# Attention and expert layer on one core: idle products and another split of work at the hand-over to the first expert

## The chip, the cores and the metric

The kernel runs on one core of a Trainium2 chip. The core has a matrix engine (TensorE, PE in the profile; its weight loads are PEld), three engines for elementwise work (VectorE or DVE, ScalarE or ACT, GpSimd or POOL), an engine that mostly issues transfers (SyncE, SP), and sixteen DMA engines that move data between device memory (DRAM) and on-chip memory (SBUF). Matrix products land in PSUM, which has eight banks. Each engine works through its own list of instructions in the order in which the program issued them; it waits at an instruction until the semaphores that the instruction names have been reached, and everything behind it waits too.

The metric is the device time of one execution in microseconds (us), lower is better.

## The reference

The reference has two parts. The first is an attention with a threshold for 8 batches, 8 heads, 576 tokens and head size 64; the second sends each of the 8 x 576 = 4608 tokens to one of 8 experts, with room for exactly 576 tokens each:

```python
scores = scale * np.matmul(q, k.transpose(0, 1, 3, 2))
thresh = np.max(scores, axis=-1, keepdims=True) - tau
scores = np.where(scores >= thresh, scores, -1000000000.0)
attn = softmax(scores)                       # exp, divided by its sum + 1e-9
x = (attn @ v) laid out as 4608 rows of 512

logits = x @ w_gate                          # 4608 x 8
# all 36864 logits in falling order: a token goes to the expert of its first
# logit whose expert still has room (576 tokens each)
for e in range(8):
    h = np.maximum(x[assigned == e] @ w1[e], 0.0)     # 512 -> 1024
    out[assigned == e] = h @ w2[e]                    # 1024 -> 512
```

## The kernel before, in words

**Attention** (lines 23 to 386) fills the first 483 us. It ends with thirty transposes of attention's result into rows of 512 values and 8 factors (`xt_unit`, lines 241 to 251; 520 values in all). PE transposes into a bank `xo`, ScalarE copies to `pp`, and SP's queue stores the rows into the DRAM tensor `xrows`. The factors are the reciprocals of the softmax sums: the rows are stored unscaled.

**The router** (class `Router`, from line 429) finds which expert fills up first and its 576 tokens, then the next, eight times. One such phase searches for a threshold in seven rounds. In each round DVE compares (`step_cmp`, tile `cmp`), PE counts (`step_cnt`, line 493), DVE copies the counts (`cn`), PE adds them (`step_flag`, line 499), DVE makes flags (`jka`), and PE turns them into the next threshold (`step_n`, lines 515 to 529). Then the expert is picked, its tokens are ranked (`rank1`, `rank2`, lines 561 to 577) and the list of the 576 rows is packed (`pack`, lines 662 to 677; tile `idx`). For the first expert nothing else is left to do beside it, which the flag `alone` marks. PE products that nobody reads are issued there by `warm` (lines 624 to 627): 20, 4 and 50 by `WARM`, all into columns 256 to 383 of the bank `rps`, which also receives the search's results. A second bank, `cps`, receives the compaction.

**The experts** (`moe`, from line 683) run one after another. Expert number r has these parts:

- `w1_load` (lines 705 to 735) loads the first weight matrix (four transfers of 128 rows of 1024 into `w1s`), on ScalarE's queue for r = 0, otherwise on SP's. The products need single passes of a rounded type, so each value is held as a high part and a low part: ScalarE makes the high part `w1h`, DVE subtracts it from the original and so makes the low part `w1l`. For r = 0 DVE makes the low parts in four groups of 128-column blocks: block 0, block 1, blocks 2 and 3, blocks 4 to 7.
- `w2_load` (lines 736 to 751) does the same for the second matrix on SP's queue (`w2s`, `w2h`, `w2l`), with the low parts put on a list of spare work for DVE (`later`, line 695).
- `rows` (lines 753 to 812) gathers the 576 rows in five blocks (four of 128, one of 64) by indirect transfers that GpSimd issues (line 759, tile `xg`), scales them by their factors (`scale`, line 762, on DVE; for r = 0 block 2 by eight ScalarE instructions, `scale_act`, line 767), transposes them on PE (`turn`, line 785), and splits the result into high and low parts (`xh` by ScalarE in line 786, `xl` by DVE in `low`, line 787).
- `ffn` (lines 814 to 884) multiplies. Layer 1 has eight blocks f of 128 hidden columns. Each needs 12 pairs of products: 4 row groups k, times high by high, low rows by high weights, high rows by low weights (line 840); a pair covers the two column halves of the 576 tokens. For r = 0 the halves are 256 and 320 tokens wide, the three kinds follow one another, and blocks 0 and 1 do their first half before either does its second, so that they can start with the first two row blocks alone. ScalarE then applies the Relu (`hf`, `H`), and DVE makes the low part of H. Layer 2 (line 872) follows, then the results are stored by indirect transfers of GpSimd (line 879), with one addition on GpSimd per expert (line 882).

**What sets the order.** A planner written in Python runs when the program is built. Each part is a generator that yields an estimated time; `run` (line 920) keeps a clock and issues, in order of the estimated times, what is due, between the products of the current expert. So the search for expert 1 is woven into the products of expert 0. Each `yield` number is such a time. The order of each engine's list is fixed by this; the waits come from the data. The tuple ("w1", 0) in `done` marks that the high parts of expert 0 are issued, ("half", 0) that two row blocks are, ("x", 0) that all are.

DVE's instructions all carry line 425, since they pass through a helper; they are told apart by their tiles.

Of the kernel before, what the change touches and what calls it, by code (L numbers as in the profile page):

```python
# [9 lines left out]
F32 = mybir.dt.float32  # L10
# [3 lines left out]
AF = mybir.ActivationFunctionType  # L14
ALU = mybir.AluOpType
# [413 lines left out]
class Router:  # L429
# [191 lines left out]
        u2=wk.tile([128,NC_],F32,name="u2"); V.scalar_tensor_tensor(u2,s.sc,BIGS+CAP,u,op0=ALU.is_lt,op1=ALU.mult)  # L621
        V.tensor_tensor(L,L,u2.unsqueeze(2).to_broadcast([128,NC_,8]),op=ALU.add)
    def close(s): s.close1(); s.close2()
    def warm(s,n):

        ps=s.ps()
        for i in range(n): s.T.matmul(ps[:,256:384],s.ones,s.tri,start=True,stop=True)
    def phase(s,last=False):

        s.stage="search"; V=s.V  # L630
        def held(t): s.pe=t; V.after(V.now+t+0.2)
        if s.first: s.prep(33)
        else:
            yield V.ease()
            s.prep()
            yield V.ease()
        s.alone=s.first; s.first=False
        if last:

            lo=s.wk.tile([128,1],F32,name="lo"); V.memset(lo,-FMAX/4); E={"lo":lo}  # L640
        else:
            E={"E":s.k("E1"),"lv":-1}
            def gap():

                w=V.wait(); s.fill()
                return w
            s.on=True
            for i in range(7):
                s.step_cmp(E); yield gap()
                held(0.34); s.step_cnt(); yield gap()  # L650
                held(0.16); s.step_flag(E["lv"]); yield gap()
                held(0.1); E=s.step_n(E)
                if not s.alone: yield V.ease()
            s.on=False
        s.pick(E)
        if last:
            yield V.wait()
            held(0.13); s.pick2()
        s.stage="pick"; s.rank1(E)
        yield V.wait()  # L660
        held(0.2); s.rank2()
# [16 lines left out]

LATS=[0.15,0.35,0.7]+[0.8]*5; FIX=(0.125,0.15)
GA=[5.0,6.5,8.0,8.0]; AGE=7.0; HALF=1; WARM=[20,4,50]  # L680
W1Y=5.0; L2O=(0,4,1,2,3); L2Z=1; HFB=3; RW=[0.2,0.4,0.4,0.4]; LOWP=(); LPF=7; LOWT=1.4; PREPW=1; WLY=(1.0,1.0)

def moe(ctx,tc,R,start,xrows,w1,w2,out,ident):
    nc=tc.nc
    V=R.V; A=nc.scalar; G=nc.gpsimd; T=nc.tensor
    E,D,F=w1.shape
# [8 lines left out]
    def later(k,g): fills.append((clk[0],k,g))  # L695
# [9 lines left out]
    def w1_load(r,s):  # L705
        while r>0 and ("w1a",r-1) not in done: yield 0.5
        q=nc.scalar if r==0 else nc.sync
        s["e"]=q.value_load(s["ei"][0:1,0:1],min_val=0,max_val=E-1)
        for k in range(4):
            t=w1p.tile([128,F],F32,name="w1s",bufs=4); s["w1s",k]=t  # L710
            q.dma_start(t,w1[ds(s["e"],1),k*128:(k+1)*128,:].rearrange("o p f -> p (o f)"))
        yield W1Y if r==0 else 5.0
        while r>0 and ("l1",r-1) not in done: yield 0.5
        s["w1h"]=w1p.tile([128,4,F],F32R,name="w1h"); s["w1l"]=w1p.tile([128,4,F],F32R,name="w1l")
        if r==0:
            for k in range(4):
                A.activation(s["w1h"][:,k],s["w1s",k],AF.Copy); yield 1.1
            done.add(("w1",0))
            for a,b in ((0,1),(1,2),(2,4),(4,8)):
                while (("row",0,1),"scaled",("row",0,4))[min(a,2)] not in done: yield 0.1  # L720
                o=slice(128*a,128*b)
                for k in range(4):
                    V.tensor_tensor(s["w1l"][:,k,o],s["w1s",k][:,o],s["w1h"][:,k,o].bitcast(F32),op=ALU.subtract)
                    if a>1: yield 0.9 if a<4 else 2.0
                for f in range(a,b): done.add(("w1l",f))
            done.add(("w1a",0))
            return
        def lowpart(k,o): V.tensor_tensor(s["w1l"][:,k,o],s["w1s",k][:,o],s["w1h"][:,k,o].bitcast(F32),op=ALU.subtract)
        for c in range(2):
            for k in range(4):  # L730
                o=slice(c*F//2,(c+1)*F//2)
                A.activation(s["w1h"][:,k,o],s["w1s",k][:,o],AF.Copy)
                yield WLY[0]
                later(("w1" if c==0 else "w1a",r) if k==3 else ("w1p",r,c,k),lambda k=k,o=o: lowpart(k,o))
                yield WLY[1]
    def w2_load(r,s):
        while ("g",r) not in done or (r>0 and ("w2",r-1) not in done): yield 0.5
        e=nc.sync.value_load(s["ei2"][0:1,0:1],min_val=0,max_val=E-1)
        for k in range(4):
            t=wk.tile([128,2,D],F32,name="w2s",bufs=4); s["w2s",k]=t  # L740
            nc.sync.dma_start(t,w2[ds(e,1),k*256:(k+1)*256,:].rearrange("o (k p) d -> p (o k) d",p=128))
        yield 5.0
        while ("w1a",r) not in done or (r==0 and ("x",0) not in done) or (r>0 and ("l2",r-1) not in done): yield 0.5
        s["w2h"]=wk.tile([128,8,D],F32R,name="w2h"); s["w2l"]=wk.tile([128,8,D],F32R,name="w2l")
        def lowpart(k,c): V.tensor_tensor(s["w2l"][:,2*k+c],s["w2s",k][:,c],s["w2h"][:,2*k+c].bitcast(F32),op=ALU.subtract)
        for k in range(4):
            for c in range(2):
                A.activation(s["w2h"][:,2*k+c],s["w2s",k][:,c],AF.Copy)
                yield WLY[0]
                later(("w2l",r,2*k+c) if 2*k+c<7 else ("w2",r),lambda k=k,c=c: lowpart(k,c))  # L750
                yield WLY[1]

    def rows(r,s):
        while r>0 and ("x",r-1) not in done: yield 0.5
        order=(4,0,1,2,3) if 0<r<=HALF else range(5)
        for t in order:
            n=128 if t<4 else 64
            x=wk.tile([128,XW],F32,name="xg",bufs=5); s["xg",t]=x
            G.indirect_dma_start(out=x[:n],out_offset=None,in_=xrows,in_offset=IOA(ap=s["idx"][:n,t:t+1],axis=0))
        s["ei2"]=wk.tile([128,1],I32,name="ei2",bufs=2); G.tensor_copy(s["ei2"],s["ei"])  # L760
        done.add(("g",r))
        def scale(t):

            n=128 if t<4 else 64
            v=s["xg",t][:n,:D].rearrange("p (h d) -> p h d",h=8)
            V.tensor_tensor(v,v,s["xg",t][:n,D:XW].unsqueeze(2).to_broadcast([n,8,64]),op=ALU.mult)
        def scale_act(t):
            x=s["xg",t]
            for h in range(8): A.activation(x[:,64*h:64*h+64],x[:,64*h:64*h+64],AF.Copy,scale=x[:,D+h:D+h+1])
        if r==0:  # L770
            step0=R.phase(); R.ahead=step0
            for _ in range(3): next(step0)
        yield GA[min(r,3)]
        while r>0 and ("l1",r-1) not in done: yield 0.5
        s["xh"]=wk.tile([128,4,576],F32R,name="xh"); s["xl"]=wk.tile([128,4,576],F32R,name="xl")
        def parts(t):
            ps=s["xps",t]
            if r==0: return (lambda n: s[n][:,:,128*t:128*t+128] if t<4 else s[n][:,:,512:576]),ps if t<4 else ps[:,:,:64]
            if t<4: return (lambda n: s[n][:,:,128*t+32*(t//2):128*t+32*(t//2)+128]),ps
            return (lambda n: s[n].rearrange("p k (a b) -> p k a b",a=2)[:,:,:,256:288]),ps[:,:,:64].rearrange("p k (a b) -> p k a b",a=2)  # L780
        def turn(t):
            n=128 if t<4 else 64
            ps=pt.tile([128,4,128],F32,name="pt"); s["xps",t]=ps
            held[0]+=0.5
            for d in range(4): T.transpose(ps[:,d,:n],s["xg",t][:n,d*128:(d+1)*128],ident[:n,:n])  # L785
            xv,pv=parts(t); A.activation(xv("xh"),pv,AF.Copy)  # L786
        def low(t):
            xv,pv=parts(t)
            V.tensor_tensor(xv("xl"),pv,xv("xh").bitcast(F32),op=ALU.subtract)
            done.add(("row",r,t))  # L790
            if t==1: done.add(("half",r))
        if r==0:


            def step(n=1):
                for _ in range(n): next(R.ahead)
            step(); scale(0); step(); turn(0); scale(1); low(0); turn(1); scale_act(2); yield V.ease()
            low(1); yield 0.25
            scale(3); scale(4); done.add("scaled"); yield 1.8
            turn(2); yield 0.6  # L800
            turn(3); low(2); yield 0.6
            turn(4); low(3); yield 0.6
            low(4); done.add("ahead")
            done.add(("x",0)); return
        scale(order[0]); yield V.wait()
        for i,t in enumerate(order):
            turn(t)
            if i<4: scale(order[i+1])
            yield max(0.8,V.wait())
            low(t)  # L810
            yield RW[min(r,3)]
        done.add(("x",r))
# [197 lines left out]
```

## Time and profile before

| | |
|---|---|
| median of 3 runs | 992.01 us (991.7 to 992.86) |
| profiled execution | 990.17 us |
| its span, first to last instruction | 988.4 us |
| PE busy | 949.5 us, 96% |
| DVE, ACT, POOL busy | 765.2, 636.3, 275.9 us |
| mean granted clock of PE | 0.990 |
| data moved | 117.01 MB, mean 118 GB/s |

A row of a timeline gives start and duration in us, the engine, the line of the kernel, the operation, output and inputs by the program's names, the shape (partitions x elements) and the number of instructions merged into the row; brackets give the idle time of the engine just before and what ended it. "SPq" and "ACTq" are transfers being issued on these queues. A row of busy time by slice gives the stretch and its length, then the busy time of each engine with its number of instructions, the granted clock of PE as a share of full speed, the busy share of the DMA engines, and GB/s. In a row of grouped instructions the columns after the bar are the total busy time and the mean duration in ns.

### The profile page before, as it was taken

To read this page: it belongs to the slowest core of one execution; us is meant where nothing else is said; L and a number is where in the kernel's file an instruction comes from. 1 tells how busy PE (TensorE), PEld (TensorE's weight loads), DVE (VectorE), ACT (ScalarE), POOL (GpSimd) and SP (SyncE) were. 2 spreads that over 40 slices of the span, in tenths; PEclk is the share of its full clock that TensorE was granted. 3 is DMA by queue.
4 is the path that set the end of the run, shared out by engine and by line. 5 is a ranking of instruction groups with operands and counts; after the bars stand their busy time and mean duration, and the time that the engine had idled before them with its cause. 6 is when DMAs were issued, how large, how long until landed. Compare 5 with 4: busy or idle time off the path is not lost.

```text
span 988.4 us, 24280 instructions
## 1 busy us (share of the span) xinstructions
PE 949.5 (96%) x9235; PEld 706.1 (71%) x9235; DVE 765.2 (77%) x2100; ACT 636.3 (64%) x1287; POOL 275.9 (28%) x460
## 2 busy tenths in 40 slices
PE   6999999999999999998889999999999999999996
PEld 4566656665666665665688797887978879898995
DVE  7999999999999999995678887686886786535220
ACT  6899899999999999996554354342543434545340
POOL 2334444443434343340110302222204023210202
PEclk9999999999999999999889999999999999999998
DMA  6231532642533333206732524151514335341101
GB/s 253 97 107 40 181 110 95 218 149 75 189 97 113 122 103 117 85 3 228 256 125 97 166 96 151 46 194 56 192 61 145 113 122 151 100 149 41 38 12 43
DMA packets 35860, 117.01 MB, mean 118 GB/s; under 512 B 4384, under 2 KB 5024, under 8 KB 35232
## 3 DMA queue, kind: packets, MB, share of 16 engines
q1 hardware_dynamic: 28352, 92.85, 27.6%
q0 software_dynamic: 5888, 19.03, 6.2%
q10 hardware_dynamic: 1504, 3.59, 1.1%
q8 instruction: 73, 1.20, 0.5%
q14 instruction: 43, 0.35, 0.1%
HBM read 93.01 MB, written 21.38 MB: 116 GB/s over the span
## 4 chain that ended last, share of the span: by engine, by line
PE 80%; DVE 8%; issue 4%; ACT 3%; DMA 3%; another core or an unknown queue 1%; POOL 0%; SPq 0%; POOLq 0%; DVEq 0%; ACTq 0%
PE pf L840 20%; PE pf L872 16%; PE sc L69 14%; PE xo L155 13%; PE tb L98 8%; PE xo L165 2%; ACT pp L86 2%; PE sc L98 1%; PE pt L785 1%; DVE z L74 1%; DVE cmp L425 1%; PE xo L177 1%; PE xo L245 1%; PE rps L493 1%; DVE pp L90 1%
## 5 line engine op out<-in xcount | busy, mean ns | idle before, releaser
L74 DVE TENSOR_SCALAR_CACHE_REDUCE z<-sc 128x576 f32<-128x576 f32 x288 | 205.6, 750 | 21.6 <-PE sc L69 10.1
L86 ACT ACTIVATE pp<-z,nb 128x576 f32<-128x576 f32 x256 | 194.3, 773 | 37.1 <-DVE z L74 33.2
L75 POOL TENSOR_SCALAR nb<-nb,taub 128x1 f32<-128x1 f32 x288 | 142.5, 496 | 258.9 <-DVE z L74 207.4
L90 DVE SCALAR_TENSOR_TENSOR pp<-z,nb,pp 128x576 f32<-128x576 f32 x256 | 200.2, 813 | 0.0
L872 PE MATMUL pf<-w2h,H 128*128 128x512 f32 x576 | 194.9, 402 | 1.2 <-issue 0.6
L69 PE MATMUL sc<-qk 64*128 64x288 f32 (+1 forms) x1280 | 179.9, 424 | 4.9 <-DVE z L74 1.7
L155 PE MATMUL xo<-pt,vt 128*64 128x320 f32 (+1 forms) x1024 | 155.9, 420 | 0.0
L116 ACT ACTIVATE pt<-tb 128x512 f32<-128x512 f32 x253 | 137.4, 590 | 0.6
L879 POOL DMA_INDIRECT out_dram<-y,idx x40 | 44.7, 1118 | 322.3 <-ACT y L875 284.2
L872 PE MATMUL pf<-w2l,H 128*128 128x512 f32 x320 | 128.7, 402 | 0.0
L872 PEld LDWEIGHTS pf<-w2h,H 128*128 128x128 f32 x576 | 106.5, 188 | 22.5 <-issue 2.5
L98 PEld LDWEIGHTS tb<-ident,pp 64*128 64x128 f32 x2032 | 74.4, 138 | 61.6 <-issue 26.4
L69 PEld LDWEIGHTS sc<-qk 64*128 64x128 f32 (+1 forms) x1280 | 92.8, 178 | 35.3 <-DVE z L74 5.9
L840 PE MATMUL pf<-xh,w1h 128*128 128x288 f32 (+2 forms) x512 | 110.2, 301 | 0.8 <-ACT xh L786 0.7
L840 PE MATMUL pf<-xl,w1h 128*128 128x288 f32 (+2 forms) x512 | 110.4, 301 | 0.0
L840 PE MATMUL pf<-xh,w1l 128*128 128x288 f32 (+2 forms) x512 | 109.9, 300 | 0.0
L875 ACT ACTIVATE y<-pf 128x512 f32<-128x512 f32 x40 | 23.9, 597 | 130.5 <-PE pf L872 127.4
L155 PEld LDWEIGHTS xo<-pt,vt 128*64 128x64 f32 x1024 | 60.6, 136 | 54.1 <-issue 27.4
L852 ACT ACTIVATE hf<-pf 128x576 f32<-128x576 f32 x56 | 36.5, 651 | 93.6 <-PE pf L840 79.1
L98 PE MATMUL tb<-ident,pp 64*128 64x64 f32 x2032 | 93.3, 229 | 3.3 <-ACT pt L116 3.0
L840 PEld LDWEIGHTS pf<-xh,w1h 128*128 128x128 f32 x512 | 82.1, 190 | 1.9 <-ACT xh L786 1.1
L840 PEld LDWEIGHTS pf<-xl,w1h 128*128 128x128 f32 x512 | 82.0, 190 | 0.1
(199 smaller groups left out, 1328.5 us busy)
## 6 DMA issues: line engine op xcount, KB each, us to landing
qk<-qk_dram SPq DMA_DIRECT2D x31, 864.0 KB, 4.7
vt<-vl_dram SPq DMA_DIRECT2D x32, 576.0 KB, 5.7
w2s<-w_dram SPq DMA_DIRECT2D x32, 512.0 KB, 5.8
w1s<-w_dram SPq DMA_DIRECT2D x28, 512.0 KB, 5.7
xrows<-pp SPq DMA_DIRECT2D x24, 260.0 KB, 2.6
xts<-xt SPq DMA_DIRECT2D x2, 1152.0 KB
pt<-xts SPq DMA_DIRECT2D x2, 1152.0 KB, 5.1
xrows<-xr SPq DMA_DIRECT2D x8, 260.0 KB, 3.4
```

The costliest lines, as they stand in the source:

```text
L69: T.matmul(sc[o,f,:HS], kd["q",h][r,c], kd["k",h][r,:],start=True,stop=True)
L74: V.tensor_scalar(z,SC.pop(t)[:,:,:HS],-0.125,None,op0=ALU.mult,op1=ALU.min,accum_out=nb[:,0:1])
L75: G.tensor_scalar(nb[:,1:2],nb[:,0:1],taub[:,0:1],None,op0=ALU.add)
L86: A.activation(pview(t),ZB[t].rearrange("p a b -> p (a b)"),AF.Exp,bias=NBI[t][:,0:1],scale=-1.0)
L90: V.scalar_tensor_tensor(pv,ZB.pop(t).rearrange("p a b -> p (a b)"),NBI[t][:,1:2],pv,op0=ALU.is_le,op1=ALU.mult,accum_out=den_of(p)[:,p%4/ ...
L98: g=slice(64*r,64*r+64); T.transpose(o[:,r],x[r%len(x)][g],ident[g,g])
L116: else: A.activation(o,tb,AF.Copy)
L155: T.matmul(xo[64*h:64*h+64,:q.stop-q.start],v[:,f,128*u+64*h:128*u+64*h+64],PT[p][:,h,u,q],start=new,stop=last,skip_group_check=True)
L840: T.matmul(ps[:,h,:n],s[w][:,k,f*128:(f+1)*128],s[x][:,k,cols[h]],start=(i==0),stop=(i==11))
L852: A.activation(hf,ps[:,:,:HS],AF.Relu)
L872: T.matmul(ps[:,0,:],H[:,f,c:c+128],s[w][:,f],start=(f==0 and j==0),stop=e)
L879: G.indirect_dma_start(out=out,out_offset=IOA(ap=s["idx"][:n,t:t+1],axis=0),in_=y[:n],in_offset=None)
```

## The change

- `warm` can be given a bank. In the phase that runs alone, 24 idle products are issued after the expert is picked, ahead of the ranking. In `rows` for r = 0, 20 idle products go to the bank `cps` after the gathers are issued, 20 before the first transposes and 10 before the second.
- The first weight load of expert 0 (ScalarE's queue) takes only the first 512 of 1024 columns of `w1`. The other 512 are loaded on SP's queue, after the gathers, ahead of `w2`. The high parts are made in two halves.
- The low parts of blocks 0 and 1 are made on DVE ahead of the scaling of row blocks 0 and 1. Blocks 2 and 3 stay on DVE after the rows. Blocks 4 to 7 (four operations of 128x512) and the low parts of expert 0's `w2` (eight of 128x512) are made on GpSimd.
- `scale_act` is gone: DVE scales all five row blocks. The order and the planned times of the row blocks change.

```diff
-    def warm(s,n):
-        ps=s.ps()
+    def warm(s,n,ps=None):
+        if ps is None: ps=s.ps()
         for i in range(n): s.T.matmul(ps[:,256:384],s.ones,s.tri,start=True,stop=True)
...
+        if s.alone: s.warm(24)
         s.stage="pick"; s.rank1(E)
...
-W1Y=5.0; ...
+W1Y=1.0; W1X=7.0; ...
...
-            q.dma_start(t,w1[ds(s["e"],1),k*128:(k+1)*128,:].rearrange("o p f -> p (o f)"))
+            c=slice(0,F//2 if r==0 else F)
+            q.dma_start(t[:,c],w1[ds(s["e"],1),k*128:(k+1)*128,c].rearrange("o p f -> p (o f)"))
...
         if r==0:
-            for k in range(4):
-                A.activation(s["w1h"][:,k],s["w1s",k],AF.Copy); yield 1.1
-            done.add(("w1",0))
-            for a,b in ((0,1),(1,2),(2,4),(4,8)):
-                while (("row",0,1),"scaled",("row",0,4))[min(a,2)] not in done: yield 0.1
+            def high(c,d):
+                for k in range(4):
+                    A.activation(s["w1h"][:,k,c],s["w1s",k][:,c],AF.Copy); yield d
+            def lows(E,a,b,d=0.0):
                 o=slice(128*a,128*b)
                 for k in range(4):
-                    V.tensor_tensor(s["w1l"][:,k,o],s["w1s",k][:,o],s["w1h"][:,k,o].bitcast(F32),op=ALU.subtract)
-                    if a>1: yield 0.9 if a<4 else 2.0
+                    E.tensor_tensor(s["w1l"][:,k,o],s["w1s",k][:,o],s["w1h"][:,k,o].bitcast(F32),op=ALU.subtract)
+                    if d: yield d
                 for f in range(a,b): done.add(("w1l",f))
+            s["lows"]=lambda f: list(lows(V,f,f+1))
+            yield from high(slice(0,F//2),0.6)
+            done.add(("w1",0))
+            while ("row",0,4) not in done: yield 0.1
+            yield from lows(V,2,4,0.9)
+            while "w1x" not in done: yield 0.1
+            yield from high(slice(F//2,F),0.8)
+            yield from lows(G,4,8,1.4)
...
+        if r==0:
+            c=slice(F//2,F)
+            for k in range(4): nc.sync.dma_start(s["w1s",k][:,c],w1[ds(e,1),k*128:(k+1)*128,c].rearrange("o p f -> p (o f)"))
...
+        if r==0: yield W1X; done.add("w1x")
...
-        def lowpart(k,c): V.tensor_tensor(s["w2l"][:,2*k+c],...)
+        def lowpart(k,c): (V if r else G).tensor_tensor(s["w2l"][:,2*k+c],...)
...
+                if r==0:
+                    lowpart(k,c); yield WLY[1]; done.add(("w2l",r,2*k+c) if 2*k+c<7 else ("w2",r)); continue
...
             for _ in range(3): next(step0)
+            R.warm(20,R.cp())
...
-            step(); scale(0); step(); turn(0); scale(1); low(0); turn(1); scale_act(2); yield V.ease()
-            low(1); yield 0.25
-            scale(3); scale(4); done.add("scaled"); yield 1.8
-            turn(2); yield 0.6
-            turn(3); low(2); yield 0.6
-            turn(4); low(3); yield 0.6
-            low(4); done.add("ahead")
+            while ("w1",0) not in done: yield 0.1
+            step(); s["lows"](0); scale(0); step(); R.warm(20,R.cp()); turn(0); s["lows"](1); scale(1); low(0); R.warm(10,R.cp()); turn(1); scale(2); low(1)
+            yield 1.3
+            turn(2); scale(3); low(2); yield 3.0
+            turn(3); scale(4); low(3); yield 1.2
+            turn(4); low(4); done.add("ahead")
```

More of the change, by code (lines that the diff above doesn't have):

```diff
@@ L680 @@
 GA=[5.0,6.5,8.0,8.0]; AGE=7.0; HALF=1; WARM=[20,4,50]
-W1Y=5.0; L2O=(0,4,1,2,3); L2Z=1; HFB=3; RW=[0.2,0.4,0.4,0.4]; LOWP=(); LPF=7; LOWT=1.4; PREPW=1; WLY=(1.0,1.0)
+W1Y=1.0; W1X=7.0; L2O=(0,4,1,2,3); L2Z=1; HFB=3; RW=[0.2,0.4,0.4,0.4]; LOWP=(); LPF=7; LOWT=1.4; PREPW=1; WLY=(1.0,1.0)
 def moe(ctx,tc,R,start,xrows,w1,w2,out,ident):
@@ L742, in w2_load, with lowpart @@
         yield 5.0
+        if r==0: yield W1X; done.add("w1x")
         while ("w1a",r) not in done or (r==0 and ("x",0) not in done) or (r>0 and ("l2",r-1) not in done): yield 0.5
         s["w2h"]=wk.tile([128,8,D],F32R,name="w2h"); s["w2l"]=wk.tile([128,8,D],F32R,name="w2l")
-        def lowpart(k,c): V.tensor_tensor(s["w2l"][:,2*k+c],s["w2s",k][:,c],s["w2h"][:,2*k+c].bitcast(F32),op=ALU.subtract)
+        def lowpart(k,c): (V if r else G).tensor_tensor(s["w2l"][:,2*k+c],s["w2s",k][:,c],s["w2h"][:,2*k+c].bitcast(F32),op=ALU.subtract)
         for k in range(4):
@@ L766, in scale @@
             V.tensor_tensor(v,v,s["xg",t][:n,D:XW].unsqueeze(2).to_broadcast([n,8,64]),op=ALU.mult)
-        def scale_act(t):
-            x=s["xg",t]
-            for h in range(8): A.activation(x[:,64*h:64*h+64],x[:,64*h:64*h+64],AF.Copy,scale=x[:,D+h:D+h+1])
         if r==0:
```

## The prediction

> **What bounds the kernel now.** I read the page first, then busy time by slice around the hand-over from attention to the first expert, then that stretch instruction by instruction, then the matmul engine's waits. Page, first lines:
>
> ```profile
> span 988.4 us, 24280 instructions
> PE 949.5 (96%) x9235; PEld 706.1 (71%) x9235; DVE 765.2 (77%) x2100; ACT 636.3 (64%) x1287; POOL 275.9 (28%) x460
> ```
>
> TensorE (PE) is busy 96% of the span, so time is won only where PE idles or runs slowly. Busy time by slice (columns: slice, length, PE, PEld, DVE, ACT, POOL busy, granted clock, DMA share, GB/s):
>
> ```profile
> 479.94:483.35 3.41, 1.98 (x27) 1.56 (x27) 1.81 (x12) 2.14 (x8) 0.00 (x0) 1.00 0.98 334
> 483.35:486.76 3.41, 2.74 (x23) 2.39 (x24) 2.90 (x10) 0.00 (x0) 0.00 (x0) 0.50 0.22 54
> 486.76:490.18 3.42, 3.42 (x52) 3.27 (x51) 2.88 (x11) 0.51 (x1) 0.00 (x0) 0.50 0.82 301
> 490.18:493.59 3.41, 2.67 (x49) 2.40 (x47) 2.82 (x6) 2.34 (x3) 2.68 (x2) 1.00 0.97 358
> 493.59:497.00 3.41, 0.92 (x8) 0.62 (x8) 1.50 (x5) 1.97 (x3) 2.50 (x4) 1.00 0.66 183
> 497.00:500.42 3.42, 2.66 (x11) 2.26 (x12) 2.20 (x7) 2.21 (x10) 1.00 (x2) 0.50 0.49 131
> 500.42:503.83 3.41, 3.08 (x17) 2.78 (x16) 2.99 (x8) 1.50 (x4) 0.00 (x0) 0.50 0.92 317
> 766.65:770.07 3.42, 2.05 (x18) 1.82 (x18) 1.29 (x6) 1.16 (x2) 1.03 (x2) 1.00 0.64 173
> 504.00:532.00 28.00, 28.00 (x264) 26.68 (x264) 25.01 (x71) 14.99 (x37) 0.00 (x0) 1.00 0.10 35
> ```
>
> The slices follow the clock, which changes only at steps of 3.41 us. It fell after slices with PE 58% busy (1.98) and 27% (0.92), stayed after 60% (766.65) and 78%, rose after 90% and 100%, and did not rise after 78% or 80%. So it is half speed from 483.35 to 490.18 and again from 497.00 to 503.83: exactly where the first expert starts. From 504 PE is never idle for 28 us.
>
> Timeline of the hand-over, and one row of the chain of waits (the second):
>
> ```profile
> 482.45 0.59 ACT L248 ACTIVATE pp<-xo 64x512 f32<-64x512 f32 x1 [0.67 <-ACT pp L249]
> 483.16 2.68 DMA xrows<-pp
> 484.48 2.29 PE L627 MATMUL rps<-trib,onesb 128*128 128x128 bf16 x20 [0.39 <-DVE scol L425]
> 488.93 3.53 PE L627 MATMUL rps<-trib,onesb 128*128 128x128 bf16 x50
> 490.61 1.22 POOL L759 DMA_INDIRECT xg<-xrows,idx  x1 [45.47 <-DMA w1s<-w_dram]
> 493.04 0.39 PE L493 MATMUL rps<-oh,cmp 128*128 128x32 bf16 x9 [0.57 <-DVE cmp L425]
> 494.95 0.69 DVE L425 TENSOR_TENSOR xg<-xg 128x512 f32<-128x512 f32 x1 [1.30 <-DMA xg<-xrows,idx]
> 495.75 0.63 PE L785 MATMUL pt<-ident,xg 128*128 128x128 f32 x4 [1.75 <-DVE jka L425]
> 496.33 0.69 DVE L425 TENSOR_TENSOR xg<-xg 128x512 f32<-128x512 f32 x1 [0.60 <-DMA xg<-xrows,idx]
> 497.07 1.11 PE L785 MATMUL pt<-ident,xg 128*128 128x128 f32 x4 [0.70 <-DVE xg L425]
> 498.87 1.22 PE L840 MATMUL pf<-xh,w1h 128*128 128x256 f32 x4 [0.69 <-ACT xh L786]
> 499.36 2.18 SPq L741 DMA_DIRECT2D w2s<-w_dram  x4
> 499.46 0.89 DVE L425 TENSOR_TENSOR w1l<-w1s,w1h 128x128 fp32r<-128x128 f32 x4
> 499.89 1.05 PE L840 MATMUL pf<-xl,w1h 128*128 128x256 f32 x4
> 500.66 1.28 DVE L425 TENSOR_TENSOR xg<-xg 128x512 f32<-128x512 f32 x2 [0.32 <-DMA xg<-xrows,idx]
> 500.75 1.05 PE L785 MATMUL pt<-ident,xg 128*128 128x128 f32 x4
> 501.81 1.05 PE L785 MATMUL pt<-ident,xg 128*128 128x128 f32 x4
> 503.41 0.62 PE L785 MATMUL pt<-ident,xg 64*128 64x64 f32 x4 [0.33 <-DVE xl L425]
> 504.43 0.64 PE L840 MATMUL pf<-xh,w1h 128*128 128x256 f32 x4
> 504.90 0.63 PE L840 MATMUL pf<-xl,w1h 128*128 128x256 f32 x4
> 505.85 0.75 PE L840 MATMUL pf<-xh,w1h 128*128 128x320 f32 x4
> ```
>
> The first expert's work starts at 498.87 and reaches its second column half at 505.85: 6.98 us for 24 products and three sets of transposes, with PE cold, waiting for scaled rows and for low parts that DVE makes late. At full clock four products start 0.47 us apart (504.43 to 504.90), cold 1.02 (498.87 to 499.89).
>
> **The change part by part.** *24 idle products before the ranking.* At full clock one costs 0.058 us: of the 50 at 488.93, the 1.25 us before 490.18 took 11 at 0.114 (2.29/20), the other 39 took the remaining 2.28. So 1.4 us. They stand ahead of attention's last four transposes, whose eviction (482.45) moves to about 483.85; the last store, and behind its landing (2.68 us after 483.16) the weight loads on ACT's queue, move as much, from 485.85 to 487.25. With half the bytes (four of 256 KB, 1.05 MB at the 358 GB/s of the 490.18 slice, 2.9 us) the halves are there and cast by about 492. Expert 0's first low parts, now ahead of scale(0) on DVE, cannot start before 494; the cover is 2 us, so this costs nothing. Ranking waits for DVE until 483.8 anyway.
>
> *20 idle products in the second bank before the search product.* They queue behind the 50, which end at 492.46, so L493 moves from 493.04 to 493.6, and DVE's reading of it to 494.05.
>
> *The row chain, on DVE.* Low part of f 0 (0.89) to 495.0; scale(0) 0.6, reading the search flags 0.25, low part of f 1 0.85, scale(1) from 496.65. Before, scale(1) began at 496.33 and its product at 498.87, 2.54 later, of which about 0.5 was transposing cold (1.11 against 0.63). So the first product comes at 498.7: nothing is won until there. The gathers themselves are issued when the index is ready, as now (490.61), and meet no weight load after about 491, so rows land before DVE asks.
>
> *From there, PE warm.* The idle 20 and 10 between transposes make the slice from 493.59 about 3.1 us busy, not 0.92. The slice from 497.00 then has 0.6 of transposes and 1.7 of products, 68%, above the 60% that stayed. 24 products by 0.118 and three sets by 0.5 (the 0.63 of 495.75 less its tail) are 4.3 us, with 0.15 for a low part: 503.15 instead of 505.85, **2.7 us won**. Scaling row block 2 on DVE, not on ACT, adds 0.6 inside this chain and is in it.
>
> *Second weight halves on SP.* Four more issues (about 0.55 us each, 2.18 for four) ahead of w2s; they start after the gathers, land near 503, and block f 4 needs them near 515. The w2 weights, 2 us later, are cast from about 513. Hidden; without that cover it would be the 2 us.
>
> *Twelve low parts from DVE to GpSimd.* This saves DVE 12 of 0.68, but PE was 28.00 of 28.00 busy there: worth nothing, at most the 1.6 us that PE idles from 532 to 570, should the search end sooner. What GpSimd costs DVE shows where it adds y rows:
>
> ```profile
> L882 POOL TENSOR_TENSOR y<-y,z 64x512 f32<-64x512 f32 x8 | 10.4, 1295 | 0.2
> 561.44 1.30 POOL L882 TENSOR_TENSOR y<-y,z 64x512 f32<-64x512 f32 x1
> 560.86 1.98 DVE L425 TENSOR_SCALAR st<-st,sm 128x136 f32<-128x136 f32 x1
> 514.41 0.28 DVE L425 TENSOR_SCALAR st<-st,sm 128x136 f32<-128x136 f32 x1
> 562.97 0.16 PE L515 MATMUL rps<-fla,hb 128*128 128x1 bf16 x1 [0.27 <-DVE jka L425]
> 750.42 2.52 DVE L425 TENSOR_TENSOR R<-th,ihl 128x720 bf16<-128x720 bf16 x2
> 752.99 0.83 PE L599 MATMUL cps<-R,poh 128*128 128x160 bf16 x9 [0.42 <-DVE R L425]
> 518.22 0.68 DVE L425 TENSOR_TENSOR w2l<-w2s,w2h 128x512 fp32r<-128x512 f32 x1
> ```
>
> DVE's operation stood until GpSimd's 1.30 us were over (1.98 against 0.28; the pair of R at 750.42 met the fourth addition), and PE then waited 0.27 and 0.42 us. Over eight such additions that is 0.09 us each. A low part has the same row length, so about 1.3 us. Bounds: 0 if all fall into DVE's free time, 12 by 1.3 = 15.6 us if PE pays each in full. I take 0.09 by 12 = **1.1 us lost**, the nearest row.
>
> The Trainium skill (SBUF — State Buffer, "Who interferes with whom") says that a DVE instruction with two SBUF inputs and a GpSimd one that reads SBUF exclude each other for the whole instruction; the 1.98 us agrees. By that rule nearly all of DVE's remaining work in this stage, comparisons and H low parts, would queue behind GpSimd, which speaks for the third rival.
>
> Sum: −2.7 + 1.1 = −1.6 us. The profiled execution took 990.17 us (span 988.4 and 1.8 around it), 1.84 below the median of the runs shown; I put the difference on the median: 992.01 − 1.6 = **990.4**.
>
> **The rivals.** *The clock stays up from 483 on* (chance 0.27). With the 24, the first slice is 88% busy instead of 58%. The slice from 483.35 becomes 60 to 63%: the 20 at L627 shrink to 1.2 us when warm. That lies between the 58% that fell and the 60% that stayed; the likeliest case takes it as fallen, since the 58% was this very stage. If it stays, the compaction's 18 products are warm (my estimate: 0.55 earlier) and the queue of 70 ends 1.0 earlier, so all behind starts 1.0 sooner: −3.7 + 1.1 = −2.6, 989.4.
>
> *The clock falls at 500.42 after all* (0.13). 68% may be too little. Then 3.41 us run at 0.47/1.02 of the speed, 1.8 us lost: −2.7 + 1.8 + 1.1 = +0.2, 992.2. The Trainium skill (TensorE: Matmul & The Clock Gate, "Part 4: PE-mode transpose") says that transposes do not count as PE being busy; by it that slice would have only 50%. The trace speaks against it: the clock rose at 503.83 after a slice made mostly of transposes (1.05 + 1.05 + part of 0.62).
>
> *GpSimd takes the port when the search needs it* (0.15, the slower side). Per block of some 3.85 us DVE wants 1.42 for the comparison and 0.82 for H, GpSimd 2.6 for two low parts: 4.84 in 3.85. Each search product stands in PE's order, so a late comparison stops all products behind it. At 0.5 us for each of twelve, 6.0 − 2.7 = +3.3, 995.3. It decides from 0.23 us each (even) and shows as slower from 0.39. For it: DVE 25.01 of 28 busy. Against it: 8.2 us of DVE work leave, and six of the eight additions cost PE nothing.
>
> *The idle products do nothing for time* (in the forecast's 0.45 as its upper edge): data, not clock, sets 505.85; then −2.7 shrinks to the 0.2 at 498.7, and GpSimd leaves +0.9, 992.9.
>
> **How the numbers follow.** Forecast 0.45, rivals 0.27, 0.13, 0.15. A measurement of this kernel tells 0.2% (2.0 us) from no change: faster is below 990.0, slower above 994.0. The forecast's own range, 989 to 992.9, lies 0.15 of its 0.45 below 990.0; with the first rival faster is 0.42. Same: 0.30 + 0.13 = 0.43. Slower 0.15. The range for 8 in 10 runs from 987.4 (clock up, search sooner by 1.6 and a little) to 994.0, leaving out most of the third rival.
>
> **What would show it.** First L840 near 498.7, the 320-column products from 503.2, four starts 0.47 apart from the first on, clock 1.00 after 490.18. Wrong: clock 0.50 after 497; L493 not later than 493.04 (then the clock stayed up); PE waits on cn, jka or H between 505 and 532 of over 2.7 us together, with comparisons well over 1.42 us; a wait at f 4 for GpSimd.

## The result and the profile after

| | before | after |
|---|---|---|
| median, side by side | 991.65 us (988.34 to 993.73, 12 runs) | 1000.52 us (996.44 to 1005.9, 12 runs) |
| ratio, 95% interval | | 1.0089 [1.0071, 1.0107] |
| profiled execution, its span | 990.17, 988.4 us | 997.92, 996.1 us |

The changed kernel is 0.9% slower: 8.9 us by the medians, 7.7 by the spans of the two profiled executions. Two executions that ran far longer than the others of their kernel (1169.09 us, of the kernel before, taken beside e5 to e8, and 3085.07 us, of e8) are left out of the ratios further down. Page of the changed kernel, first lines:

```profile
span 996.1 us, 24441 instructions
PE 952.4 (96%) x9309; PEld 708.6 (71%) x9309; DVE 768.9 (77%) x2089; ACT 635.3 (64%) x1283; POOL 294.0 (30%) x472
```

VectorE lost twelve subtractions to GpSimd and is busier than before (768.9 against 765.2 us), with eleven instructions fewer. That is the first sign. The hand-over itself went about as forecast. Busy time by slice of the changed kernel, columns as in the prediction:

```profile
486.76:490.18 3.42, 3.23 (x71) 3.06 (x68) 3.18 (x13) 0.18 (x1) 0.18 (x1) 1.00 0.50 174
...
497.00:500.42 3.42, 1.53 (x11) 1.30 (x11) 2.49 (x4) 1.19 (x2) 0.31 (x2) 1.00 0.46 142
...
503.62:537.90 34.28, 28.67 (x249) 26.68 (x248) 25.59 (x54) 17.59 (x43) 18.00 (x12) 0.95 0.18 66
```

And its timeline:

```profile
490.00 1.22 POOL L774 DMA_INDIRECT xg<-xrows,idx  x1 [45.05 <-DMA w1s<-w_dram]
...
492.43 0.39 PE L493 MATMUL rps<-oh,cmp 128*128 128x32 bf16 x9
...
498.58 0.74 PE L852 MATMUL pf<-xh,w1h 128*128 128x256 f32 x4 [1.54 <-ACT xh L799]
...
503.62 0.75 PE L852 MATMUL pf<-xh,w1h 128*128 128x320 f32 x4
...
551.53 0.93 POOL L774 DMA_INDIRECT xg<-xrows,idx  x1 [4.17 <-issue]
```

The last of these rows is expert 1's first gather; in the kernel before it is this:

```profile
542.94 0.93 POOL L759 DMA_INDIRECT xg<-xrows,idx  x1 [2.00 <-issue]
```

The granted clock stays at 1.00 until 528.76. The first product starts at 498.58, the second column half at 503.62 instead of 505.85: 2.2 us won. Then it is lost in one stage. From the second column half to expert 0's layer 2 PE took 26.8 us before (505.85 to 532.68) and takes 34.3 now (503.62 to 537.91), of which it is busy for 28.67. Expert 1's gathers begin at 551.53 instead of 542.94; GpSimd, which issues them, had been idle for 4.17 us by then, so its own work does not hold them up.

VectorE's and GpSimd's operations grouped by shape in the stretch from 503 to 545 (after the bar: total us, mean ns, idle time before), first of the kernel before, then of the changed one:

```profile
L425 DVE SCALAR_TENSOR_TENSOR cmp<-st,sd,b 128x1152 bf16<-128x1152 f32 x4 | 5.7, 1418 | 0.1
L425 DVE TENSOR_TENSOR H<-hf,H 128x512 fp32r<-128x512 f32 x8 | 5.5, 681 | 0.0
L425 DVE TENSOR_TENSOR w2l<-w2s,w2h 128x512 fp32r<-128x512 f32 x8 | 5.4, 678 | 0.0
...
L425 DVE TENSOR_TENSOR H<-hf,H 128x64 fp32r<-128x64 f32 x8 | 1.7, 218 | 0.0
```

```profile
L425 DVE TENSOR_TENSOR H<-hf,H 128x512 fp32r<-128x512 f32 x8 | 10.3, 1286 | 0.0
L425 DVE SCALAR_TENSOR_TENSOR cmp<-st,sd,b 128x1152 bf16<-128x1152 f32 x4 | 7.9, 1981 | 0.1
L425 DVE TENSOR_TENSOR H<-hf,H 128x64 fp32r<-128x64 f32 x8 | 3.9, 485 | 0.0
...
L758 POOL TENSOR_TENSOR w2l<-w2s,w2h 128x512 fp32r<-128x512 f32 x8 | 13.4, 1692 | 12.2 <-ACT w2h L761 12.2
L724 POOL TENSOR_TENSOR w1l<-w1s,w1h 128x512 fp32r<-128x512 f32 x4 | 5.5, 1394 | 10.4 <-ACT w1h L720 10.4
```

On average a low part of H takes 1286 ns instead of 681, a comparison 1981 instead of 1418, and GpSimd's own subtraction 1394 (`w1`) and 1692 (`w2`). Twelve subtractions of 0.68 us, 8.2 us, left VectorE; H and the comparisons alone grew by 4.8 (8 x 0.605) + 2.2 (5.7 to 7.9) + 2.2 (the 64-column H, 1.7 to 3.9) = 9.2 us. PE pays, since each search product has its place in PE's order and everything behind it waits. The chain of waits of the changed kernel runs through these operations (start, us), and the timeline shows GpSimd beside them:

```profile
509.62 2.38 DVE H L425 x2
512.08 2.86 DVE H L425 x2
...
523.90 2.39 DVE cmp L425
...
535.08 2.54 DVE cmp L425
```

```profile
507.70 5.46 POOL L724 TENSOR_TENSOR w1l<-w1s,w1h 128x512 fp32r<-128x512 f32 x4 [10.39 <-ACT w1h L720]
...
512.14 0.16 PE L529 MATMUL rps<-fla,onesb 128*128 128x1 bf16 x1 [1.11 <-DVE jka L425]
...
516.50 0.39 PE L493 MATMUL rps<-oh,cmp 128*128 128x32 bf16 x9 [1.70 <-DVE cmp L425]
...
535.11 3.64 POOL L758 TENSOR_TENSOR w2l<-w2s,w2h 128x512 fp32r<-128x512 f32 x2 [4.57 <-ACT w2h L761]
...
537.67 0.39 PE L493 MATMUL rps<-oh,cmp 128*128 128x32 bf16 x9 [0.87 <-DVE cmp L425]
```

PE's waits in this stage, changed kernel (engine, tile, line, what it waited for: us, times, longest):

```profile
PE rps L493 <- DVE cmp L425: 3.0, 3, 1.7
PE rps L499 <- DVE cn L425: 1.5, 2, 0.9
PE rps L529 <- DVE jka L425: 1.1, 1, 1.1
```

5.6 us of waits and a clock fall among them (one step of 3.41 us at half speed from 528.76, 1.7 us of work) make 7.3 of the 7.5 us.

### The profile page after: what moved, and what is told of

It is laid out like the page before. It is cut to its first block, busy times and chain, and to the rows that moved or that the text cites. A ratio compares the mean times of both kernels' runs of the same rounds, so it can differ in the third digit from the quotient of the medians.

```text
span 996.1 us, 24441 instructions
## 1 busy us (share of the span) xinstructions
PE 952.4 (96%) x9309; PEld 708.6 (71%) x9309; DVE 768.9 (77%) x2089; ACT 635.3 (64%) x1283; POOL 294.0 (30%) x472
## 4 chain that ended last, share of the span: by engine, by line
PE 80%; DVE 8%; issue 4%; ACT 3%; DMA 2%; SPq 0%; POOLq 0%; ACTq 0%; DVEq 0%
PE pf L852 19%; PE pf L884 17%; PE sc L69 14%; PE xo L155 12%; PE tb L98 8%; PE xo L165 2%; DVE cmp L425 2%; ACT pp L86 2%; PE pt L798 2%; PE sc L98 1%; PE rps L493 1%; DVE H L425 1%; DVE z L74 1%; DMA out_dram<-y,idx 1%; PE xo L177 1%
## 5 line engine op out<-in xcount | busy, mean ns | idle before, releaser
L864 ACT ACTIVATE hf<-pf 128x576 f32<-128x576 f32 x56 | 36.5, 651 | 98.5 <-PE pf L852 84.8
L155 PEld LDWEIGHTS xo<-pt,vt 128*64 128x64 f32 x1024 | 60.6, 136 | 54.1 <-issue 27.4
```

What stands on the lines that cost most here:

```text
L155: T.matmul(xo[64*h:64*h+64,:q.stop-q.start],v[:,f,128*u+64*h:128*u+64*h+64],PT[p][:,h,u,q],start=new,stop=last,skip_group_check=True)
L864: A.activation(hf,ps[:,:,:HS],AF.Relu)
```

## The experiments

The theory to test was that GpSimd's subtractions shut VectorE out (theory P in the expectations). The rivals: PE or VectorE wait for GpSimd's results as data (W); the place of the search for expert 1 in PE's list (O); chance of the clock (C). To compare executions that start some us apart, the table counts from expert 0's first gather to the starts of rows of the timeline (us), one profiled execution each; the ratio is to the kernel before, run on the same chip in turn. Where a kernel was run twice (e1 and e10, e5 and e14, e9 and e15), its stretch from the second column half to layer 2 repeats within 0.1 us; by expert 1's layer 2 the two executions lie 1.6 to 5.3 us apart.

| kernel | second column half | layer 2 of expert 0 | first gather of expert 1 | layer 1 of expert 1 | its layer 2 | ratio [95%] |
|---|---|---|---|---|---|---|
| before | 15.2 | 42.1 | 52.3 | 76.5 | 105.7 | 1 |
| after | 13.6 | 47.9 | 61.5 | 83.0 | 113.8 | 1.0089 [1.0071, 1.0107] |
| e1 all low parts on VectorE | 13.6 | 39.5 | 56.1 | 77.6 | 114.3 | 1.0045 [1.0029, 1.0062] |
| e10 e1 again | 13.6 | 39.5 | 56.1 | 74.0 | 109.0 | 1.0039 [1.0007, 1.0071] |
| e2 w2's on GpSimd | 15.9 | 45.1 | 60.1 | 79.0 | 115.1 | 1.0039 [1.0018, 1.0060] |
| e3 w1's on GpSimd | 13.6 | 41.6 | 55.5 | 76.9 | 108.3 | 0.9997 [0.9983, 1.0011] |
| e4 before, low parts on GpSimd | 20.0 | 50.1 | 59.5 | 83.5 | 112.8 | 1.0043 [1.0026, 1.0060] |
| e5 e1, search earlier | 13.0 | 40.4 | 53.6 | 74.7 | 104.0 | 0.9988 [0.9978, 0.9998] |
| e11 e5 with a smaller shift | 15.2 | 41.6 | 55.6 | 78.6 | 107.8 | 1.0001 [0.9979, 1.0023] |
| e12 e5 with a larger shift | 13.6 | 43.9 | 53.9 | 77.4 | 106.7 | 0.9991 [0.9965, 1.0016] |
| e14 e5 again | 14.2 | 41.6 | 54.9 | 76.6 | 105.9 | 0.9965 [0.9949, 0.9982] |
| e6 after, search earlier | 12.8 | 52.7 | 62.1 | 84.8 | 114.0 | 1.0046 [1.0028, 1.0064] |
| e7 e5, GpSimd reads beside | 13.5 | 53.3 | 67.5 | 88.5 | 117.8 | 1.0119 [1.0096, 1.0142] |
| e8 e5, GpSimd writes beside | 13.3 | 41.1 | 54.3 | 75.4 | 104.7 | 1.0006 [0.9990, 1.0021] |
| e9 e5 without idle products | 15.5 | 42.9 | 56.2 | 79.1 | 108.4 | 0.9954 [0.9932, 0.9977] |
| e15 e9 again | 15.3 | 42.6 | 55.9 | 77.5 | 106.8 | 0.9975 [0.9960, 0.9989] |
| e16 e15 with the 24 | 15.2 | 42.5 | 55.7 | 77.4 | 106.7 | 0.9966 [0.9950, 0.9983] |
| e13 before, with the idle products | 17.0 | 43.9 | 54.1 | 77.8 | 107.0 | 1.0012 [0.9992, 1.0032] |

### Which low parts cost: e1 to e4

In `w1_load` and in `w2_load`, r = 0 (e1 both edits, e2 the first, e3 the second; e4 makes the opposite edits in the kernel before):

```diff
-            yield from lows(G,4,8,1.4)
+            yield from lows(V,4,8,2.0)
...
-        def lowpart(k,c): (V if r else G).tensor_tensor(...)
+        def lowpart(k,c): V.tensor_tensor(...)
...
-                if r==0:
-                    lowpart(k,c); yield WLY[1]; done.add(...); continue
                 later(...,lambda k=k,c=c: lowpart(k,c))
```

> The changed kernel with all twelve low parts (blocks 4 to 7 of w1, all of w2) back on VectorE, planned as before. Theory 'port': GpSimd's additions of about 1.3 us hold back VectorE's two-input operations and PE stands behind them; without them the stretch from the second column half (503.6) to layer 2 takes again what it took before (505.85 to 532.54, 26.7 us, against 34.3 in the changed kernel), the 2.2 us won at the start stay, and the time is 1.5 to 3 us below before. Rival 'hand-over': idle products, weight halves and the row order cost the time; then it stays 5 us or more above before.

> The changed kernel with only the four low parts of w1's blocks 4 to 7 back on VectorE; the eight of w2 stay on GpSimd. Theory 'port': each GpSimd operation costs PE about the same (7.6 us by twelve, 0.63 each), so about 2.5 us of the loss go and the kernel lies 5 to 6 us above before. If the four operations that follow one another without a gap are the costly ones (PE waits of 1.1 and 1.7 us stand beside them in the changed kernel), it lies only 3 to 4 above before.

> The changed kernel with only the eight low parts of w2 back on VectorE, by the list of spare work; the four of w1 stay on GpSimd. Theory 'port': about 5 us of the loss go, 1 to 3 us above before. Rival 'the four are the costly ones': 4 to 6 us above before. The two halves of the loss should add up to about that of the changed kernel.

> The kernel before with only the twelve low parts moved to GpSimd. Theory 'port': 5 to 9 us slower than before, with PE waits for cmp, cn and jka between 508 and 540, and VectorE's comparisons of 1.42 us stretched to 2.4 or more. Rival 'hand-over': within 2 us of before.

In the stage itself theory P holds. With all low parts back on VectorE, e1 takes 25.9 us from second column half to layer 2, the changed kernel 34.3: 8.4 us, 0.70 for each of the twelve. In e3, which leaves four on GpSimd, it takes 28.0.

In the whole time the expectations were missed, and the parts do not add up. e1 was 0.45% slower than before, where it should have been faster, though with e10 it reaches layer 2 earlier than any other kernel here. e2 lost 0.39%, less than theory P gave it, and e4 0.43%, a little less than the 5 us that it gave at the least; e4's second column half is already 4.8 us late. e3 lost nothing: giving the eight low parts of `w2` back to VectorE takes off the whole loss, giving back all twelve only half of it. So GpSimd was not all.

One place where e1 loses is in the table: its gathers for expert 1 begin 56.1 us after expert 0's, 3.8 later than before. In e1 the search's first product, L493, stands as follows; the second row is that of the kernel before:

```profile
508.88 0.39 PE L493 MATMUL rps<-oh,cmp 128*128 128x32 bf16 x9
```

```profile
507.47 0.39 PE L493 MATMUL rps<-oh,cmp 128*128 128x32 bf16 x9
```

Counted in PE's list, that product comes behind 11 products of the second column half in the kernel before, behind 38 in e1 and in the changed kernel; the last product of the seven rounds at L515 behind 160, 183 and 174. The planner issues the products earlier against the search than it did. In e3 the first search product also stands behind 38 and the gathers come at 55.5, yet e3 is no slower than before; so the late search alone does not explain e1's loss. In e1 VectorE then waits for search products while PE works ahead of it (its waits from second column half to expert 1's gathers, in e1; columns as above):

```profile
DVE cn L425 <- PE rps L493: 2.7, 4, 1.1
DVE scol L425 <- PE rps L572: 1.4, 1, 1.4
DVE ob L425 <- PE cps L599: 1.3, 1, 1.3
DVE w1l L425 <- ACT w1h L720: 1.0, 1, 1.0
```

The wait for `cn` is not among those of the kernel before. The 1.0 us for `w1h` is the second weight half, cast later. e1's profile also has two clock falls of 6.83 us, at 556.06 and 573.12. Hence rivals O and C.

### The search's place, and GpSimd's port: e5 to e8

In `ffn`, one line (in e5 on e1, in e6 on the changed kernel); it puts the first search product behind 15 products of the half:

```diff
             if hs==(1,): yield ("x",r)
+            if r==0 and (f,hs)==(0,(1,)): yield 3.0
```

e7 and e8 are e5 with `extra` called at the twelve places where the changed kernel has GpSimd's subtractions (x the weights, h their high part; t is read by nobody; e8 has the last line in place of the one above it):

```diff
+    def extra(x,h):
+        t=wk.tile([128,512],F32,name="gx",bufs=1)
+        G.tensor_tensor(t,x,h.bitcast(F32),op=ALU.subtract)
+        G.tensor_copy(t[:,0:1],h[:,0:1].bitcast(F32)); G.memset(t,0.0)
```

> All twelve low parts on VectorE, and the second column half of expert 0's products planned 3.0 us later, so that the first search product of expert 1 stands behind 15 products of that half in PE's order (38 in e1, 11 before) and the last one behind 160 (178 in e1, 150 before). Theory O (the search of expert 1 stands too far back in PE's order, so VectorE idles 4 us of the 42.5 between the second column half and expert 1's gathers): that idle time falls to about 1 us, the gathers begin at 541 to 543 instead of 545.96, expert 1's layer 1 begins by 565 instead of 567.5, and the time is 988.5 to 991, no slower than before. Rival C (the loss of e1 comes from the clock's two falls, which chance decides): the gathers may come sooner, the time stays at 995 to 998.

> The changed kernel with the same 3.0 us shift of the second column half and nothing else. Theory P (GpSimd's low parts lengthen VectorE's two-input operations, and that sets this stage): H pairs still 2.4 us and comparisons 2.4 us where a low part runs on GpSimd, at least 32 us from the second column half to layer 2, and 995 to 998. Theory O alone (the order is what the changed kernel loses by): 989 to 992, with VectorE's operations as short as before.

> e5 and, beside it, the twelve subtractions on GpSimd as well, into a tile that nobody reads, at the places where the changed kernel has them; VectorE still makes the low parts that are used. Nothing waits for GpSimd's results but the next writes of the weight tiles. Theory P: pairs of H and comparisons of over 2 us come back, the stage from the second column half to layer 2 takes 33 us or more (e5 about 26), the time is at least 5 us above e5's. Rival W (the changed kernel loses because PE or VectorE wait for GpSimd's results as data): within 1 us of e5.

> As e7, but in place of each extra subtraction GpSimd copies one column (to tie it to the same place) and then fills the 128x512 unread tile with zeros, so that it writes as much and reads next to nothing. Theory P in the form that GpSimd's reading is what shuts VectorE out: VectorE's operations as in e5, within 1 us of e5's time. Theory P in the form that any access of GpSimd does: operations lengthened by the length of the fill, at least 2 us above e5.

These four ran on one chip, with medians of 983.14 (e5), 989.13 (e6), 996.97 (e7) and 984.27 us (e8); the kernel before had 983.54 there.

e6 against e5 is the price of GpSimd's low parts, with the same added line in both: 6.0 us, 0.5 for each of twelve. It includes what the clock takes: e6's profile has falls of 6.83 and 3.41 us in this stage, e5's none. e7 against e5 settles why. Nothing that anybody reads comes from GpSimd there, and VectorE does all its work, yet the kernel is 13.8 us slower, the largest loss of all; W would have had it within 1 us. What PE waits for is the comparisons (PE's waits from second column half to layer 2, first e7, then e5):

```profile
PE rps L493 <- DVE cmp L425: 8.3, 3, 4.9
```

```profile
PE rps L493 <- DVE cmp L425: 0.7, 1, 0.7
```

e8 writes 512 columns just as often and leaves VectorE's operations with two tiles as they were (grouped operations from 503 to 545, first e7, then e8; the last row of each is GpSimd's):

```profile
L425 DVE TENSOR_TENSOR w2l<-w2s,w2h 128x512 fp32r<-128x512 f32 x7 | 7.9, 1133 | 0.0
L425 DVE SCALAR_TENSOR_TENSOR cmp<-st,sd,b 128x1152 bf16<-128x1152 f32 x4 | 7.4, 1859 | 0.1
L425 DVE TENSOR_TENSOR H<-hf,H 128x512 fp32r<-128x512 f32 x7 | 6.7, 962 | 0.0
...
L708 POOL TENSOR_TENSOR gx<-w2s,w2h 128x512 f32<-128x512 f32 x8 | 12.4, 1546 | 18.1 <-issue 10.6 <-ACT w2h L765 7.3
```

```profile
L425 DVE SCALAR_TENSOR_TENSOR cmp<-st,sd,b 128x1152 bf16<-128x1152 f32 x4 | 5.7, 1418 | 0.1
L425 DVE TENSOR_TENSOR w2l<-w2s,w2h 128x512 fp32r<-128x512 f32 x8 | 5.5, 682 | 0.0
L425 DVE TENSOR_TENSOR H<-hf,H 128x512 fp32r<-128x512 f32 x8 | 5.4, 677 | 0.0
...
L708 POOL MEMSET gx<- 128x512 f32 x12 | 6.3, 527 | 0.7
```

With the fills, a low part of H takes 677 ns and a comparison 1418 on average, as when GpSimd does nothing; with the subtractions 962 and 1859. The fills are shorter (527 ns against 1.3 us and more), but several lie wholly inside a VectorE operation and do not lengthen it: the H at 522.60 takes 0.68 us around a fill from 522.67 to 523.20. The Trainium skill (SBUF — State Buffer, "Who interferes with whom") says just this: a VectorE instruction with two inputs in SBUF contends with a GpSimd instruction that reads SBUF, and not with one that only writes it. The 677 and 1418 ns with the fills agree. One operation of another kind took longer beside a fill: `E`, which reads one tile and single values per partition, took 0.66 us at 503.88 in e8, where a fill ran from 503.97 to 504.50, and 0.24 us in e5, where none ran.

e5 against e1 is the order: one line, and the same work. Gathers for expert 1 come 53.6 us after expert 0's instead of 56.1 (54.9 in e14), and the time goes from 1.0045 to 0.9988 of before, by about 5.6 us of 990. The expected gather time of 541 to 543 was not reached in absolute time, since this execution began late (a clock fall in attention); its gathers of expert 0 are at 492.27. In e6 the same line takes the changed kernel from 1.0089 to 1.0046, although its first stage becomes longer: half of what the changed kernel loses goes with this line.

### Chance of the clock, and other shifts: e10 to e12

> e1 once more, unchanged, on the same chip as e11 and e12. Theory O: slower than before by 0.3 to 0.6% again, expert 1's gathers about 47.5 us behind the first product, PE waits of over 4 us from layer 2 of expert 0 to layer 2 of expert 1. Rival C (chance of the clock, or of this one chip): within 0.2% of before and of e11.

> e5 with the second column half planned 2.0 us later in place of 3.0 (first search product behind 22 products, the last behind 162). Theory O gives a time between e1's and e5's if what counts is how early the search stands, and as good as e5 or up to 1 us better if 15 products is already too early for VectorE's first comparison.

> e5 with 4.0 us (first search product behind 8 products, the last behind 148, as in the kernel before). PE then waits for the first comparison (about 1 us), and the gathers of expert 1 begin up to 1.5 us sooner: within 1 us of e5, to either side.

e11 and e12 are e5 with `yield 2.0` and `yield 4.0` in place of `yield 3.0`.

e10, the same program as e1, is slower than before by 0.39% again. Its profile has the clock at 1.00 from 6 to 982 us and the gathers at 56.1 us as in e1. So the late gathers come from the order, and the falls in e1 came on top. But rival C is not put aside by this. The profiled execution of e10 took 990.13 us, no more than the kernel before (median 991.81). Of the ten executions of e10, the three with a mean granted clock of 0.996 or 0.997 took 987.76 to 992.78 us, the seven with 0.986 to 0.992 took 992.91 to 1001.75. The loss in the median is that of the executions in which the clock fell more. The executions of e3, with the search nearly as late, had 0.990 to 0.997, those of e14, with the search moved forward, 0.993 to 0.998. So the added line brings earlier gathers and a clock that falls less, and the runs do not part the two; why the clock falls more in e1's order stays open.

e11 (2.0 us) and e12 (4.0 us) cannot be told from e5, and with all three no loss against before is left.

### The idle products: e9, e13 to e16

e9 and e15 are e5 without them; e16 puts the 24 back; e13 puts all of them into the kernel before, at the same places. The expectations speak of 30 in the second bank; it is 50:

```diff
-        if s.alone: s.warm(24)
...
             for _ in range(3): next(step0)
-            R.warm(20,R.cp())
...
-            step(); ...; step(); R.warm(20,R.cp()); turn(0); ...; low(0); R.warm(10,R.cp()); turn(1); ...
+            step(); ...; step(); turn(0); ...; low(0); turn(1); ...
```

> e5 without the change's new idle products (24 ahead of the ranking, 20 and 10 in the second bank), the same order otherwise. If the idle products are worth what the forecast gave them: the clock falls twice between 485 and 505, the second column half begins 2 to 3 us later after the first gather than in e5, and the time is 2 to 3 us above e5's, slower than before. If the hand-over is set by gathers and VectorE: within 0.7 us of e5.

> The kernel before with only the new idle products (24 ahead of the ranking, 20 and 10 in the second bank between the search product and the transposes); order, weights' loads and low parts as before. If the idle products are worth their 2 us and the search's place in PE's order is what eats them in e1: 1 to 2 us faster than before (ratio 0.998 to 0.999). If they cost as much later as they bring (a delayed start of the weight loads, clock falls at dearer places): no faster than before, with single runs far above the median.

> e5 unchanged, on one chip with e13, e15 and e16. Ratio 0.998 to 1.000, as on the other chip.

> e9 unchanged (e5 without the new idle products). If leaving them out really helps: ratio 0.994 to 0.997, at least 1.5 us below e14, and no single run far above the median. If e9's lead was the spread of the runs: within 1 us of e14.

> e9 with the 24 idle products ahead of the ranking put back, the 30 in the second bank left out. If the 24 are what costs: at e14's time; if the 30 are: at e15's. By the clock alone it stays up through the compaction (about 0.5 us won) and falls from 497 on.

e9 was expected to be slower than before. The second column half comes 2.5 us later than in e5, as expected, but the time came out at 0.9954 [0.9932, 0.9977]. e15, the same program beside e14, had 0.9975 with e14 at 0.9965: the first lead was spread. e14 itself was faster than the expected 0.998 to 1.000. e14, e15 and e16 have medians of 986.49, 987.45 and 987.17 us and cannot be told apart. By the table the idle products bring the second column half 1.1 us forward (e14 against e15, 14.2 and 15.3), and the difference is still 0.9 at expert 1's layer 2; a time difference of 1.0 us is as much, but lies inside the spread. Nor is the 1.1 a firm figure: with all idle products the half begins at 13.0 to 15.2 (e5, e11, e12, e14), without them at 15.3 and 15.5. In the kernel before they bring nothing (e13). Its profile shows why that can be: the clock fell all the same, at the one slice in which rows were late (busy time by slice):

```profile
495.06:498.48 3.42, 0.78 (x11) 0.63 (x9) 1.28 (x4) 1.69 (x2) 2.26 (x4) 1.00 0.82 247
498.48:501.89 3.41, 2.72 (x19) 2.32 (x17) 1.44 (x4) 1.89 (x6) 0.00 (x0) 0.50 0.53 170
```

None of the kernels with the low parts on VectorE alone and the search moved forward is measurably slower than the kernel before; e9, e14, e15 and e16 are faster, by 0.25 to 0.46%. Up to expert 1's layer 2 the table gives e14 no lead (105.9 against 105.7); it comes in the stages behind. There the planned order differs, and one more difference is on record: the profile of the kernel before has three stalls of VectorE (described in the last section), behind which PE waits 1.74, 1.37 and 1.05 us; the profiles of e9, e14, e15 and e16 have none. How much of the lead is this was not tried.

## Why the prediction was wrong, step by step

- *24 idle products ahead of the ranking*: right, at no cost. More than that, the clock stayed up from 483, as the first rival had it, and the index came 0.6 us sooner (that rival had 1.0). In e16, which has the 24, the clock is 1.00 until 494.87; in e9, without them, it falls at 483.45.
- *20 in the second bank push L493 to 493.6*: no, it is at 492.43, since the 50 ahead of it ran warm.
- *The row chain; first product at 498.7*: right, 498.58.
- *2.7 us won at the second column half*: 2.2 (503.62 against 503.15 forecast). Mechanism right, size nearly.
- *Second weight halves on SP, hidden*: right for PE. With VectorE making the low parts it costs VectorE a wait of 1.0 us (e1).
- *Twelve low parts: 1.1 us lost*. **This term failed.** It measures 6.0 us (e6 against e5), 0.5 each, where 0.09 was taken; in its own stage 8.4 (after against e1). The third rival had the mechanism and, with 0.5 each, the price. The 0.09 was a mean over eight additions of which six cost PE nothing at the places where they fall. The twelve fall into a stage where VectorE was busy for 25.01 of 28 us, some 22 of them with operations on two tiles (comparisons and low parts, grouped from 504 to 532); in the changed kernel eleven of the twelve ran beside such an operation. The row of 1.98 us that the prediction took as its sign is not of this kind: `st` is made from one tile and single values per partition, as `E` is, and e8's `E` took longer beside a mere fill. The pair of R is of this kind. The argument "8.2 us of DVE work leave" was wrong for the same reason: 9.2 came back.
- *"worth nothing, at most the 1.6 us ... should the search end sooner"*, and a sum that carries the 2.7 through to the end. **This second step failed too**, and no rival named it. That PE was busy for 28.00 of 28.00 us does not say that a stage moves as a block: expert 1's search, on VectorE, runs beside expert 0's products, and what it needs from PE stands in PE's order. The planner's list moved 27 products ahead of the first search product. PE finished its products sooner and expert 1's rows came later: e1 wins 2.6 us up to layer 2 and is 3.8 behind at expert 1's gathers. Moving the search forward again gives back 4 to 6 us (e1 to e5, after to e6), fewer clock falls included. The third rival's 995.3 was too low by about this.
- *Clock rule of the slices (58% falls, 60% stays)*: does not hold as a rule. On the changed kernel's own steps, 3.41 us apart, with PE busy for 1.84 and 2.05 of them:

```profile
494.62:498.04 3.42, 1.84 (x18) 1.45 (x18) 2.03 (x9) 0.71 (x2) 2.25 (x3) 1.00 0.73 197
525.34:528.76 3.42, 2.05 (x24) 1.59 (x23) 3.03 (x6) 2.53 (x6) 2.80 (x2) 1.00 0.00 0
528.76:532.17 3.41, 3.41 (x17) 3.26 (x16) 2.15 (x3) 0.00 (x0) 1.78 (x2) 0.50 0.00 0
```

  It stayed up after 54% and fell after 60%. What else decides was not found. By the rule the clock should have fallen after the first of these rows, in the middle of the hand-over; that it did not was luck.

Together: GpSimd's low parts 4 to 6 us, the search's place with the clock falls that go with it 4 to 6, less some 1 to 2 for the earlier start, against a measured loss of 8.9. This is no clean sum, since the price of the one depends on the other: e3, with four low parts on GpSimd and the search late, lost nothing, and e1, with none on GpSimd, lost 0.45%. That GpSimd's reading holds VectorE up, and PE behind it, is shown by e7 and e8; how the rest parts between late gathers and the clock stays open.

## What to carry to other kernels

In this kernel, work moved from VectorE to GpSimd was no relief, because VectorE's remaining operations read two tiles. Price such a move at the place where it will run and against the operations that another engine waits for, not at the mean over other places. Where a planner weaves a search into products, look after each edit at how many products stand ahead of each search product; a start that PE alone wins can be handed back at the next thing that the other engine makes. Idle products that keep the clock up are worth what the waiting engine then does with it, and here that was about 1 us at most, inside the spread. Where executions of one kernel spread widely, set their times beside their granted clocks before calling a difference that of the order.

## What the runs showed of the hardware that was not expected

A stall without a visible cause. In several profiles, of the kernel before too, VectorE stands for 2 to 4 us at an instruction whose inputs are there by the profile. First e1, then the kernel before:

```profile
554.54 0.15 DVE L425 TENSOR_SCALAR_CACHE_REDUCE jka<-rps 32x8 bf16<-32x8 f32 x1 [3.49 <-remote]
...
554.76 0.16 PE L529 MATMUL rps<-fla,onesb 128*128 128x1 bf16 x1 [2.48 <-DVE jka L425]
```

```profile
607.02 0.19 DVE L425 CAST cn<-rps 128x32 fp32r<-128x32 f32 x1 [3.85 <-remote]
```

In both, the product that it reads is drawn 3 us earlier, but the record of PE's semaphore step stands right before the row (554.52, 607.00). Both fall among the gathers of the next expert. In e1 the clock fell behind it, at 556.06. Such stalls of over 2 us stand in the profiles of the kernel before, e1 to e4 and e10 to e13, in none of the changed kernel, e5 to e9 and e14 to e16. It is not the chip alone, since e9 to e16 ran on one chip. The cause stays open.
